# First chunk of all batches as two pairs, loaded two tokens a partition in 512-byte packets

## The chip, the core and the metric

One core of a Trainium2 chip runs the whole program. Its engines run side by side, each with its own queue that is worked off in order: TensorE (PE) multiplies matrices and writes to PSUM, VectorE (DVE) and ScalarE (ACT) work element by element, GpSimd (POOL) here issues most of the loads and some constants, and SyncE (SP) issues the stores and the transposing transfers. Sixteen DMA engines move the data that all of them ask for. The metric is the device time of one execution in microseconds (us); lower is better.

## What is computed

Two things in a row. First a retention layer without softmax on q, k, v of shape 8 x 8 x 576 x 64 (batches, heads, tokens, head size), then a two-layer network with the exact GELU on the 4608 tokens of 512 features.

```python
scores = scale * np.matmul(q, k.transpose(0, 1, 3, 2))
gamma = 1.0 - 2.0 ** (-5.0 - np.arange(H, dtype=np.float32))
Dmat = np.where(rel >= 0, gamma[:, None, None] ** rel[None, :, :], 0.0)   # rel = row - column
attn = np.matmul(scores * Dmat, v)
x = attn.transpose(0, 2, 1, 3).reshape(B * S, H * D)
h = x @ w_in                                  # 512 x 2048
out = (0.5 * h * (1.0 + erf(h / sqrt(2)))) @ w_out   # 2048 x 512
```

Inputs and output are fp32; the kernel multiplies in bf16.

## The kernel before

**Attention in chunks.** The 576 tokens of a batch are cut in four chunks of 128 and a tail of 64. Because the decay is a power of the distance, a chunk needs only its own scores and a state: the sum of k times v over all earlier chunks, 64 x 64 for each head. A *unit* is one chunk of one batch; two batches make a pair (`bp`), and units of a pair at the same chunk form a *group* that uses the four 64 x 64 quarters of TensorE side by side. For a unit the steps are: load q, k and v; transpose q and k (`qkT`, on TensorE by `turn` for the first groups, by a DMA in `turn_dma` for the later ones); scores k by q (`scores`, `sc`); the product with the mask, and in the first chunk with the decay too (`masked`, `ret`); the inner product with v (`inner`, `o_ps`); the product of the state with q (`cross`); the state itself (`state`, `u_ps`, copied to `u_sb`), which needs v scaled by the decay (`scaled_v`, `vh`); and the copy from PSUM to `xT` (`evacuate`), the input of the network.

**The first chunk** has no state before it. It multiplies its scores by `near`, a table of decay for each head (eight Exp activations of ScalarE on the distances `far`), and its inner product takes v as loaded, without scaling. Units 0 to 3 are the first chunk of the first four batches, and each is a group by itself (`groups = [[0], [1], [2], [3]]`). Their scores use TensorE in two halves, and their x is ready one after the other.

**The network in blocks** of 512 tokens. Block 0 consists of units 0 to 3. `mlp1` makes hT (w_in by x, 16 pieces of 128 features), ScalarE applies the GELU into `g`, `mlp2` multiplies by w_out (`oT`) for block 0. Later blocks use Strassen-like schemes with seven products (`part`, `m`; and from block 6 on `fast`, `f` for the first product too) on sums of w_in, w_out, g and x that VectorE makes. Blocks 0 and 1 may work on parts of a block: in block 0 the cuts are 0, 128, 256, 384, 512 tokens, one for each unit.

**Weights.** w_in comes in eight pieces of 256 columns (wi0 to wi7), w_out in eight pieces of 256 rows (wo0 to wo7). All are cast to bf16 by the DMA, and so are q, k and v, which is why GpSimd issues them. Only the very first loads (q and k of unit 0) go over the hardware queues of SP and ACT as fp32, into `first`, and are cast on VectorE. A load of one unit has 128 tokens on 128 partitions and eight heads of 64 numbers, so packets of 256 bytes on the side of the source.

**What sets the order.** The list `ORDER` (L330) gives the loads in the order in which GpSimd issues them (k1 is k of unit 1, `io` the two iotas, `dq2` a table of decay made on GpSimd), and, with letters a, b, s, z, p, u, due times and choices for the later units. At most eight loads are under way. A planner written in Python (`T`, `on`, `pe`, `fire`, and the loop at L1190) keeps an estimated time for each engine and emits each engine's instructions in the order in which it expects them to be ready; on the chip each engine then simply runs its list in order. Before its time 16, where it expects a gap on TensorE, it emits filler matmuls on zeros (`warm`). ACT makes `near`, then dv, dqT and the table load of the GELU before block 0's first activation.

Of the kernel before, what the change touches and what calls it, by code (L numbers as in the profile page):

```python
# [17 lines left out]
def kernel(  # L18
# [23 lines left out]
    C = 128  # L42
# [10 lines left out]
    groups = [[0], [1], [2], [3]]  # L53
# [9 lines left out]
    kept = pair_of[1, 0]  # L63
    raw = [i for i in range(N_U) if units[i][1] == 0]
    v_order = [i for i in range(N_U) if i not in kept]
    n = v_order.index(pair_of[0, NCI - 2][0])
    v_order[n:n] = kept

    N_PE_TR = 7
    HW_FIRST = ((("q", 0),), (("k", 0),))  # L70
# [39 lines left out]
    first = {}  # L110
    for n, keys in enumerate(HW_FIRST):
        t = o_pool.tile([128, 2, H, D], FP32, tag=f"o{n}", name="first")
        for x, (what, i) in enumerate(keys):
            first[what, i] = t[:, x]
            src = {"q": q, "k": k, "v": v}[what][2 * units[i][0] + units[i][2]]
            (nc.sync, nc.scalar)[n].dma_start(t[:, x], src[:, 0:C, :].rearrange("h s d -> s h d"))
# [14 lines left out]
    far = const.tile([128, 1, 128], FP32, name="far")  # L131
    ident = const.tile([128, 1, 128], BF16, name="ident")
    near = const.tile([128, 2, HP, 128], FP32, tag="near", name="near")
# [8 lines left out]
    def constants():  # L142
        nc.gpsimd.iota(val[:, 0, :], pattern=[[1, 128]], base=0, channel_multiplier=-1,
                       allow_small_or_imprecise_dtypes=True)
        nc.gpsimd.iota(pos[:, 0, :], pattern=[[C, NCI]], base=0, channel_multiplier=1,
                       allow_small_or_imprecise_dtypes=True)
        at = on("pool", 0.45)
        nc.vector.tensor_scalar(far, val, 0.0, 1.0e6, op0=ALU.is_lt, op1=ALU.mult)
        nc.vector.tensor_tensor(far, far, val, op=ALU.add)
        far_at = on("dve", 0.55, at)  # L150
        nc.vector.tensor_scalar(ident, val, 0.0, None, op0=ALU.is_equal)
        on("dve", 0.35)
        for h in NEAR[:N_NEAR]:
            make_near(h)
            on("act", 0.306, far_at + 0.05)

    def make_near(h):
        nc.scalar.activation(near[:, h % 2, h // 2], far[:, 0, :], AF.Exp, scale=log_gamma[h], bias=ln_scale)

    N_NEAR, NEAR = 5, (0, 2, 4, 6, 1, 3, 5, 7)  # L160
    ident1 = ident[:, 0, :]

    def make_args():
        nc.vector.tensor_scalar(pos[TAIL:, :, NCI - 1:], pos[TAIL:, :, NCI - 1:], float(-TAIL), None, op0=ALU.add)
        nc.vector.tensor_tensor(pe_arg, lgh.to_broadcast([128, H, NCI]), pos.to_broadcast([128, H, NCI]), op=ALU.mult)
        nc.vector.tensor_tensor(off, lgT, pos[:, :, 1:2].to_broadcast([128, HP, 1]), op=ALU.mult)
# [4 lines left out]
    def make_dq(hp):  # L171
        nc.scalar.activation(dqT[:, hp, C:2 * C], val[:, 0, :], AF.Exp, scale=lgT[:, hp], bias=off[:, hp])
        dq_at[1] = T["act"] + 0.41

    dq_at = {}
    later = [(4.0, "act", 0.306, lambda h=h: make_near(h)) for h in NEAR[N_NEAR:]]
    later += [(5.6, "dve", 0.45, make_args), (11.0, "dve", 0.6, make_msk),
             (6.0, "act", 0.3, lambda: nc.scalar.activation(dv, pe_arg, AF.Exp, scale=-1.0, bias=ln_scale))]
    later += [(6.2, "act", 0.41, lambda hp=hp: make_dq(hp)) for hp in range(HP)]
    later += [(8.0, "act", 1.45, lambda: nc.scalar.activation(warm_act, ln_scale, AF.Gelu))]  # L180
    T["act"], T["dve"], T["pool"] = 2.8, 2.05, 0.85


    queued = []
# [3 lines left out]
    def sum_w(i):  # L188
# [7 lines left out]
        ws_at[i] = on("dve", 1.05, land_out[i]) + SEM  # L196
# [3 lines left out]
    MOVE = {"wi": 1.33, "wo": 1.42, "ld": 0.89, "short": 0.44, "turn": 1.88, "store": 0.9}  # L200
# [47 lines left out]
    dq_done = {1}  # L248
# [23 lines left out]
    def tiles_of(i):  # L272
        g = groups[group_of[i]]
        if i not in loaded:
            if i < 4:
                qk = const.tile([128, 2, H, D], BF16, name=f"qk{i}")
            elif i == g[0]:
# [3 lines left out]
            pool, more = (const, str(i)) if i < 4 else (ld_pool, "")  # L281
            loaded[i] = (qk, pool.tile([128, H, D], BF16, tag="v" + more, bufs=1 if i < 4 else N_V, name="v_ld"))
        return loaded[i]

    def load(what, i):
# [24 lines left out]
        qk, v_ld = tiles_of(i)  # L310
        src = {"q": q, "k": k, "v": v}[what]
        for jj in (j,) if j is not None else range(2):
# [3 lines left out]
            else:  # L316
                dst = qk[:, "qk".index(what)] if i < 4 else qk[0:n, "qk".index(what), :, jj]
# [7 lines left out]
    for x, keys in enumerate(zip(*HW_FIRST)):  # L325
        for n, (what, i) in enumerate(keys):
            land[what, i] = (4.6, 5.2)[n] + 0.75 * x
            t = tiles_of(i)
            cast_due[what, i] = (t[1] if what == "v" else t[0][:, "qk".index(what)], first[what, i])
    ORDER = ("wi1 k1 wi0 io q1 v0 q2 k2 v1 wi2 v2 k3 wi3 q3 v3 wi4 wi5 wi6 k4 q5 k5 q4 v5 wi7 wo1 wo0 k6 v4 dq2 "  # L330
# [7 lines left out]
             "b21+6.0").split()  # L338
# [9 lines left out]
    for n, g in enumerate(groups):  # L348
        ORDER += [what + str(i) for what in "qkv" for i in g if what + str(i) not in ORDER and (what, i) not in first]

    def v_free(i):
        return "Bdone" in st[i] if i in raw else "V" in st[i]
# [16 lines left out]
    def finish_later():  # L369
        while later:  # L370
            _, engine, dur, fn = later.pop(0)
# [49 lines left out]
    DRAIN = 0.25  # L421
    SEM = 0.12
# [43 lines left out]
    def qkT_of(n):  # L466
        s = sg[n]
        if "qkT" not in s:
            if n < 4:
                s["qkT"] = tr_pool.tile([128, 2, HP, 128], BF16, tag="qkT1", bufs=2, name="qkT")  # L470
            else:
                s["qkT"] = tr_pool.tile([128, 2, H, 128], BF16, tag="qkT", bufs=N_QKT, name="qkT")
        return s["qkT"]

    def turn(n, jj, half):
        qk, qkT = loaded[groups[n][0]][0], qkT_of(n)
        pe_waits(max(land["qk"[jj], i] for i in groups[n]))
        b, t = bank([128, HP, 128], BF16, "qk_ps", False)
        rows = TAIL if units[groups[n][0]][2] is None else C
        for x in range(HP):  # L480
            what = qk[:, jj, 2 * x:2 * x + 2, :] if n < 4 else qk[:, jj, HP * half + x, :, :]
            nc.tensor.transpose(t[:, x, 0:rows], what[0:rows], ident1[0:rows, 0:rows])  # L482
        done = pe(0.225, HP)
        done = either(0.42 * rows / C, done, qkT[:, jj, HP * half:HP * half + HP, 0:rows], t[:, :, 0:rows])
        release(b, done + 0.05)
        sg[n]["T"] = max(sg[n].get("T", 0.0), done + SEM)

# [19 lines left out]
    def scores(n):  # L507
# [3 lines left out]
        if n < 4:  # L511
            got = [bank([128, HP, 128], FP32, "sc") for _ in range(2)]
            for hp in range(HP):
                for e in range(2):
                    sl = slice(64 * e, 64 * e + 64)
                    nc.tensor.matmul(got[e][1][:, hp, :], lhsT=qkT[sl, 1, hp, :], rhs=qkT[sl, 0, hp, :],
# [831 lines left out]
```

## Time and profile before

| what | us |
|---|---|
| median of three runs | 286.79 (285.31 to 288.63) |
| span of the profiled execution, first to last instruction | 283.7 |
| time of the profiled execution beyond its span | not given by the page |
| filler matmuls in front (10 + 23) | 4.4 + 6.0 busy |
| loads that GpSimd issues | mostly 0.85 to 0.93 each |
| DMA packets | 152804, of which 141120 are under 512 bytes on the side that the profile counts |

In the profile, lines start with the source line (L701) and engine; `hT<-xT,w_in` is what an instruction writes and reads; a number of instructions stands after x. In the chain of waits each step is followed back to what released it. In the view by stretch each row has the stretch, its length, then the busy time and number of instructions of PE, PE's weight loads, DVE, ACT and POOL, the granted TensorE clock (1.00 is full), the DMA share and GB/s.

### The profile page before, as it was taken

The numbers are of one execution on the slowest core, as the hardware profiler recorded it, in microseconds if no ns is written. First come the engines' busy times: TensorE is split into PE (matmuls) and PEld (weight loads), VectorE is DVE, ScalarE is ACT, GpSimd is POOL, SyncE is SP. The second block draws the span as 40 slices with busy tenths as digits, with TensorE's granted clock in tenths as the row PEclk, the third lists the DMA queues.
The fourth block names the chain that finished last, engine by engine and source line by source line (L and its number), as shares of the span: only waits on it lengthen the run. The fifth ranks groups of instructions, "written<-read, shape, count | busy, mean of one in ns | idle before, by whom it ended". The sixth has DMA issues, their size and how long they took to land.

```text
span 283.7 us, 8075 instructions
## 1 busy us (share of the span) xinstructions
PE 278.0 (98%) x3361; PEld 207.6 (73%) x3361; DVE 199.7 (70%) x412; ACT 158.8 (56%) x362; POOL 114.0 (40%) x143
## 2 busy tenths in 40 slices
PE   8989999999999999999999999999999999999994
PEld 3577666688874588548855778558888888888894
DVE  5753483979865595898178867889669968966822
ACT  5676724755456635693298874564565374665320
POOL 8979987993364465625468552000000000000000
PEclk9999999999999999999999999999999999999999
DMA  9999999999999999999999999910003000400133
GB/s 150 165 182 173 188 180 163 146 142 147 172 161 195 190 147 128 156 229 149 135 197 203 147 137 150 222 21 2 0 2 128 23 2 0 151 0 2 74 114 111
DMA packets 152804, 35.39 MB, mean 125 GB/s; under 512 B 141120, under 2 KB 148928, under 8 KB 152768
## 3 DMA queue, kind: packets, MB, share of 16 engines
q0 software_dynamic: 116832, 18.10, 95.3%
q1 hardware_dynamic: 34528, 16.26, 32.9%
q10 hardware_dynamic: 1408, 0.52, 0.7%
q8 instruction: 26, 0.43, 0.7%
q14 instruction: 10, 0.08, 0.1%
HBM read 36.70 MB, written 9.44 MB: 163 GB/s over the span
## 4 chain that ended last, share of the span: by engine, by line
PE 92%; POOL 3%; DMA 3%; issue 0%; DVE 0%; POOLq 0%
PE m L885 35%; PE hT L701 29%; PE f L966 13%; PE oT L746 5%; PE o_ps L600 3%; PE sc L535 3%; DMA w_in<-in_moe_w_in_dram 3%; POOL qk L318 2%; PE o_ps L653 1%; PE u_ps L619 1%; PE qk_ps L482 1%; POOL v_ld L318 1%; POOL w_in L291 1%; PE sc L525 0%; PE o_ps L591 0%
## 5 line engine op out<-in xcount | busy, mean ns | idle before, releaser
L701 PE MATMUL hT<-xT,w_in 128*128 128x512 bf16 (+3 forms) x560 | 87.4, 312 | 0.8 <-DMA w_in<-in_moe_w_in_dram 0.8
L710 ACT ACTIVATE g<-hT 128x512 bf16<-128x512 f32 (+2 forms) x106 | 57.7, 556 | 36.9 <-PE hT L701 36.1
L701 PEld LDWEIGHTS <-w_in 128*128 128x128 bf16 x560 | 48.4, 98 | 33.8 <-DMA w_in<-in_moe_w_in_dram 1.0
L885 PEld LDWEIGHTS <-gs 128*128 128x128 bf16 x656 | 62.2, 98 | 7.7
L885 PE MATMUL m<-w_sum,gs 128*128 128x256 bf16 (+1 forms) x400 | 47.7, 268 | 0.0
L318 POOL DMA_DIRECT2D v_ld<-in_v_dram x40 | 34.0, 854 | 19.3 <-DMA qk_ld<-in_k_dram 8.8
L318 POOL DMA_DIRECT2D qk_ld<-in_k_dram x36 | 30.4, 851 | 21.7 <-DMA qk_ld<-in_q_dram 19.1
L558 DVE TENSOR_TENSOR ret<-sc,msk 128x512 bf16<-128x512 f32 x48 | 30.2, 683 | 12.2 <-PE sc L535 12.2
L318 POOL DMA_DIRECT2D qk_ld<-in_q_dram x36 | 30.4, 851 | 16.9 <-DMA qkT<-qk_ld 6.5
L885 PE MATMUL m<-w_out,gs 128*128 128x256 bf16 x256 | 32.5, 273 | 0.0
L885 PE MATMUL m<-w_sum,g 128*128 128x256 bf16 x256 | 30.9, 273 | 0.0
L572 ACT ACTIVATE vh<-v_ld,dv 128x64 bf16<-128x64 bf16 x120 | 30.0, 339 | 0.0
L782 DVE TENSOR_TENSOR gs<-g 128x1024 bf16<-128x1024 bf16 x32 | 21.8, 686 | 9.0 <-ACT g L710 8.2
L885 PEld LDWEIGHTS <-g 128*128 128x128 bf16 x256 | 24.9, 98 | 3.9
L991 ACT ACTIVATE g<-f 128x512 bf16<-128x512 f32 x36 | 20.2, 590 | 8.9 <-PE f L966 7.5
L786 DVE TENSOR_TENSOR gs<-g 128x1024 bf16<-128x1024 bf16 x32 | 21.6, 684 | 0.0
L672 DVE TENSOR_TENSOR xT<-o_ps,dqT 128x512 bf16<-128x512 f32 (+1 forms) x32 | 18.4, 617 | 4.5 <-PE o_ps L653 4.4
L966 PEld LDWEIGHTS <-w_in 128*128 128x128 bf16 x192 | 18.8, 98 | 2.2
L461 ACT CAST u_sb<-u_ps 128x512 bf16<-128x512 f32 x15 | 8.7, 587 | 16.0 <-PE u_ps L619 16.0
L461 ACT COPY o<-m 128x512 f32<-128x512 f32 x14 | 8.2, 587 | 15.7 <-PE m L885 15.7
L987 ACT ACTIVATE g<-p 128x512 bf16<-128x512 f32 x12 | 7.6, 630 | 14.1 <-DVE p L985 14.1
L966 PEld LDWEIGHTS <-wi 128*128 128x128 bf16 x144 | 14.0, 98 | 1.6
(96 smaller groups left out, 337.6 us busy)
## 6 DMA issues: line engine op xcount, KB each, us to landing
out_dram<-o SPq DMA_DIRECT2D x27, 256.0 KB, 6.3
v_ld<-in_v_dram POOLq DMA_DIRECT2D x32, 128.0 KB, 9.1
qk_ld<-in_k_dram POOLq DMA_DIRECT2D x28, 128.0 KB, 10.7
qk_ld<-in_q_dram POOLq DMA_DIRECT2D x28, 128.0 KB, 8.6
w_in<-in_moe_w_in_dram POOLq DMA_DIRECT2D x8, 256.0 KB, 7.3
w_out<-in_moe_w_out_dram POOLq DMA_DIRECT2D x8, 256.0 KB, 8.0
out_dram<-o SPq DMA_DIRECT2D x14, 128.0 KB, 2.1
qk_ld<-in_q_dram POOLq DMA_DIRECT2D x8, 64.0 KB, 11.4
```

Source lines behind the costliest of these rows:

```text
L318: nc.gpsimd.dma_start(dst, src[2 * bp + jj, :, ci * C:ci * C + n, :].rearrange("h s d -> s h d"))
L461: nc.scalar.copy(dst, src)
L558: nc.vector.tensor_tensor(r, t, by, op=ALU.mult)
L572: nc.scalar.activation(vh[:, h, :], loaded[i][1][:, h, :], AF.Copy, scale=dv[:, h, ci:ci + 1])
L672: nc.vector.tensor_tensor(x_of(i)[:, :, n * x:n * x + n], o, dqT[:, :, ci * C:ci * C + n], op=ALU.mult)
L701: nc.tensor.matmul(hT[:, m, :], lhsT=w[:, cc, o:o + 128], rhs=x_tiles[t][:, cc, lo:hi], start=(cc == 0), stop=(cc == N_DM - 1))
L710: nc.scalar.activation(g_of(t, m0 // 2)[:, m0 % 2:m0 % 2 + n, lo:hi], hT, AF.Gelu)
L782: nc.vector.tensor_tensor(s.rearrange("p m a b -> p m (a b)"), g[:, :, 0, :], g[:, :, 1, :], op=ALU.add)
L786: nc.vector.tensor_tensor(s, g[:, :, :, LEFT], g[:, :, :, RIGHT], op=MINUS)
L885: nc.tensor.matmul(m[:, 0 if apart else ts, :], lhsT=a, rhs=w[:, c0:c1], start=p in begins and mm == 0 and ts == 0, stop=mm == N_DF // 2 - ...
L966: nc.tensor.matmul(m[:, y, :], lhsT=a[:, c], rhs=d[:, c], start=p in (P1, P7) and y == 0 and c == 0, stop=c == 1, skip_group_check=True)
L991: nc.scalar.activation(g[:, :, rows, cols], m, AF.Gelu)
```

## The change

Units 0 to 3 become two groups of a pair each. Each unit is loaded with two adjacent tokens to a partition, so 64 partitions by eight heads by 512 bytes, and the two batches of a pair lie in the two halves of the partitions. q and k of both batches of the first pair go ahead over the hardware queues of SP and ACT as fp32 (four loads for two), all else by GpSimd. Everything in the first chunk then works on tokens split by parity:

- transposes take 64 x 64 outputs in column halves, 64 for 32; scores take 64 x 64 quarters, 64 instructions of 128 columns for 32 over half the array; the inner product has 64 as before; the state has 64 for 32, since each parity is a product of its own
- `near` has three 64-wide blocks of distances for each head (`away`), eight activations of 192 columns for 128, and a table `dv2` is added; `masked_two` makes four masked products for a pair, as many as before
- v of a pair is scaled in place by one VectorE instruction of 1024 columns, after the inner product has read it
- `evacuate` writes xT with a stride of two tokens
- block 0 is cut in two halves of 256 tokens; dqT starts from chunk 0, so GpSimd makes three of these tables instead of two
- the list of loads, and all due times and choices behind it, are new. In the built program ScalarE scales v for 9 later units where it did so for 15 units, and VectorE for the rest; in the last three blocks VectorE has 5 copies to `p` (2 before), 9 to `f` (8) and 3 to `o` (2).

```diff
-    groups = [[0], [1], [2], [3]]
+    groups = [[0, 1], [2, 3]]
...
-    N_PE_TR = 7
+    N_PE_TR = 5
...
+    def doubled(what, i):
+        src = {"q": q, "k": k, "v": v}[what][2 * units[i][0] + units[i][2]]
+        return src[:, 0:C, :].rearrange("h (p t) d -> p h (t d)", t=2)
...
+    first = [o_pool.tile([128, H, 2, D], FP32, tag=f"o{n}", name="first") for n in range(2)]
+    for n, what in enumerate("qk"):
+        for i in range(2):
+            (nc.sync, nc.scalar)[i].dma_start(first[n][half_of(i)].rearrange("p h t d -> p h (t d)"), doubled(what, i))
...
-    ORDER = ("wi1 k1 wi0 io q1 v0 q2 k2 v1 wi2 v2 k3 wi3 q3 v3 wi4 wi5 wi6 k4 q5 k5 q4 v5 wi7 wo1 wo0 k6 v4 dq2 "
...
+    ORDER = ("v0 io v1 wi0 q2 k2 q3 k3 wi1 v2 v3 wi2 wi3 k4 wo0 q11 wi5 wi4 q4 q5 k5 dq1 wi6 wi7 k6 wo1 wo2 v5 wo3 "
...
+        if n < P0:
+            got = [[bank([128, HP, 2, 64], FP32, "sc") for _ in range(2)] for _ in range(2)]
             for hp in range(HP):
+                for kp in range(2):
+                    for j in range(2):
+                        cols = slice(64 * j, 64 * j + 64)
+                        for e in range(2):
+                            sl = slice(64 * e, 64 * e + 64)
+                            nc.tensor.matmul(got[kp][e][1][cols, hp], lhsT=qkT[sl, 1, 2 * hp + kp, cols],
+                                             rhs=qkT[sl, 0, 2 * hp:2 * hp + 2, cols],
+                                             start=(hp == 0), stop=True, skip_group_check=True)
...
+                nc.vector.tensor_tensor(vh, vh, dv2.to_broadcast([128, H, 2, D]), op=ALU.mult)
...
+        if pair[0] < 4:
             for j, i in enumerate(pair):
+                sl = half_of(i)
+                for h in range(H):
+                    for t in range(2):
+                        nc.tensor.matmul(u_ps[sl, h, :], lhsT=loaded[i][0][sl, 1, h, t, :], rhs=st[i]["vh"][sl, h, t, :],
+                                         start=(h == 0 and t == 0), stop=(h == H - 1 and t == 1), skip_group_check=True)
...
-            x_at[i] = either(0.68, s["B"], x_of(i), o) + SEM
+            x_at[i] = either(0.68, s["B"], x_of(i).rearrange("c h (p t) -> c h t p", t=2), o) + SEM
...
-            cuts = (0, 128, 256, 384, 512) if t == 0 else (0, 256, 512)
+            cuts = (0, 256, 512)
```

In the built program TensorE's list after the change runs: 10 fillers, the first pair's transposes, 6 fillers, its scores, 7 fillers, the second pair's transposes of q, 2 fillers, of k, the first pair's inner product, 4 fillers, the second pair's scores, hT of the first 256 tokens with wi0, wi1, wi2, the first pair's state, the second pair's inner product, hT with wi3, two oT matmuls that read wo0, hT of the second 256 tokens with wi0 to wi3, and hT of all 512 tokens with wi4, wi5, wi6, wi7 with 16 transposes of the next group in between.

More of the change, by code (lines that the diff above doesn't have):

```diff
@@ L310, in load @@
         qk, v_ld = tiles_of(i)
+        if i < 4:
+            dst = (v_ld if what == "v" else qk[:, "qk".index(what)])[half_of(i)]
+            nc.gpsimd.dma_start(dst.rearrange("p h t d -> p h (t d)"), doubled(what, i))
+            sw_dma(0.94, "two", putter(land, (what, i)))
+            return
         src = {"q": q, "k": k, "v": v}[what]
@@ L476, in turn @@
         qk, qkT = loaded[groups[n][0]][0], qkT_of(n)
-        pe_waits(max(land["qk"[jj], i] for i in groups[n]))
+        pe_waits(turn_at(n, jj, half))
         b, t = bank([128, HP, 128], BF16, "qk_ps", False)
@@ L486, in turn, with turn_at @@
         sg[n]["T"] = max(sg[n].get("T", 0.0), done + SEM)
+    def turn_at(n, jj, half):
+        if not ident_at or n == 0 and ("qk"[jj], half) not in cast_at or any(("qk"[jj], i) not in land for i in groups[n]):
+            return 1e9
+        at = cast_at["qk"[jj], half] if n == 0 else max(land["qk"[jj], i] for i in groups[n]) + 0.05
+        return max(at, ident_at[0])
     def turn_dma(n, jj):
@@ L542, in masked @@
         s = st[i]
-        if i not in raw and any(x[3] is make_msk for x in later):
+        if i < 4:
+            if i % 2 == 0:
+                masked_two(i)
+            return
+        if not made(make_msk):
             finish_later()
@@ L584, in inner @@
         s = st[i]
-        pe_waits(max(s["R"], s["V"] if "vh" in s and i not in raw else land["v", i]))
+        if i < 4:
+            if i % 2 == 0:
+                inner_two(i)
+            return
+        pe_waits(max(s["R"], s["V"]))
         if j is None:
@@ L1287 @@
                 turn(*a)
-                half = (half + 1) % (2 if nT < 4 else 4)
+                half = (half + 1) % 4
                 nT += half == 0
```

286 lines of the change are left out of this document (173 added, 113 removed), and 14 rows, old and new, of the table ORDER.

## The prediction

> **What bounds the kernel now.** I read the page first: busy shares and the chain that ended last.
>
> ```profile
> PE 278.0 (98%) x3361; PEld 207.6 (73%) x3361; DVE 199.7 (70%) x412; ACT 158.8 (56%) x362; POOL 114.0 (40%) x143
> PE 92%; POOL 3%; DMA 3%; issue 0%; DVE 0%; POOLq 0%
> ```
>
> TensorE is the bound, with 6% of the chain on GpSimd's DMA issues and on one DMA. A share is an average, so the second view is busy time by stretch (the first number after the stretch is its length, the next PE's busy time).
>
> ```profile
> 0.00:18.50 18.50, 16.53 (x170) 9.36 (x171) 11.72 (x42) 12.30 (x33) 16.50 (x25) 1.00 1.70 162
> 18.50:32.20 13.70, 13.70 (x168) 10.45 (x168) 3.83 (x8) 8.91 (x20) 12.16 (x15) 1.00 1.83 181
> 180.00:240.00 60.00, 60.00 (x717) 49.30 (x717) 49.12 (x90) 32.89 (x58) 0.00 (x0) 1.00 0.15 40
> 280.00:283.70 3.70, 0.01 (x1) 0.00 (x0) 0.29 (x1) 0.00 (x0) 0.00 (x0) 0.82 0.49 139
> ```
>
> From 18.5 on PE never pauses; a busy PE can hide short waits, but the chain confirms that it is PE's own work. The last 3.7 us are the last store. So whatever can be gained lies before 18.5, and anything lost later is lost in full. The chain in order of time (start, length, what) shows the start and gives the pace of PE's groups.
>
> ```profile
> 1.25 0.88 POOL w_in L291
> 11.04 7.39 DMA w_in<-in_moe_w_in_dram
> 18.47 1.05 PE hT L701 x8
> 27.88 0.89 PE qk_ps L482 x16
> 32.29 0.57 PE sc L535 x32
> 40.28 4.37 PE hT L701 x40
> 44.65 0.86 PE oT L746 x4
> 120.16 8.74 PE hT L701 x40
> ```
>
> The start is GpSimd issuing loads until 11.0, then the fourth piece of w_in landing at 18.4. In front of it PE runs filler matmuls:
>
> ```profile
> L1180 PE MATMUL warm<-zeros 128*128 128x512 bf16 x23 | 6.0, 382 | 0.0
> ```
>
> From 18.47 the remaining 261.5 us of PE work and 3.7 us of store are fixed. My milestone is the end of block 0's first matrix product (hT) for all 512 tokens and all of w_in, 32.2 now (the chain's sc at 32.29 follows it). The change is worth what it moves that milestone, plus or minus work carried across it.
>
> **What the loads cost.** GpSimd's rows (start, length) and the DMA view of the same issues (last number: us from issue to landing) give landings:
>
> ```profile
> 10.17 0.93 POOL L318 DMA_DIRECT2D qk<-in_k_dram  x1
> 11.78 0.96 POOL L318 DMA_DIRECT2D qk<-in_q_dram  x1
> 12.66 0.95 POOL L318 DMA_DIRECT2D v_ld<-in_v_dram  x1
> 13.52 2.33 POOL L291 DMA_DIRECT2D w_in<-in_moe_w_in_dram  x3
> 42.22 0.69 POOL L318 DMA_DIRECT2D qk_ld<-in_q_dram  x1
> 43.44 0.68 POOL L318 DMA_DIRECT2D qk_ld<-in_q_dram  x1 [0.53 <-DMA w_out<-in_moe_w_out_dram]
> ```
> ```profile
> first<-in_k_dram ACTq DMA_DIRECT2D x1, 256.0 KB, 4.6
> first<-in_q_dram SPq DMA_DIRECT2D x1, 256.0 KB, 4.0
> w_in<-in_moe_w_in_dram POOLq DMA_DIRECT2D x1, 256.0 KB, 5.0
> qk<-in_k_dram POOLq DMA_DIRECT2D x1, 128.0 KB, 5.5
> w_in<-in_moe_w_in_dram POOLq DMA_DIRECT2D x1, 256.0 KB, 7.4
> qk<-in_q_dram POOLq DMA_DIRECT2D x1, 128.0 KB, 6.9
> v_ld<-in_v_dram POOLq DMA_DIRECT2D x1, 128.0 KB, 6.8
> w_in<-in_moe_w_in_dram POOLq DMA_DIRECT2D x1, 256.0 KB, 7.2
> qk_ld<-in_q_dram POOLq DMA_DIRECT2D x1, 64.0 KB, 7.1
> qk_ld<-in_q_dram POOLq DMA_DIRECT2D x1, 64.0 KB, 6.4
> ```
>
> The first software load lands at 1.25+5.0 = 6.25. Further on: k of unit 3 at 15.67, wi3 at 18.44, q at 18.68, v at 19.46, wi4 at 20.72. In a backlog a 128 KB load therefore takes 0.78 (19.46-18.68) and a 256 KB piece of w_in 1.26 (20.72-19.46). Between 15.67 and 18.68 one of each landed in 3.01 where 2.04 would do: about 1.0 us was lost there, and I keep that loss. The two 64 KB half-height loads land at 49.32 and 49.84, 0.52 apart.
>
> **The change, part by part.**
>
> *New loads.* No row shows 64 partitions by 8 heads of 512 bytes. The half-height load has the same number of packets and half the bytes (0.52), the w_in piece the same packets and twice the bytes (1.26); the old load has the same bytes in twice the packets (0.78). A straight line in bytes gives 0.77, so the packet size alone buys little; I take 0.72, with 0.52 and 1.26 as ends. Issuing one costs GpSimd 0.69 (half height) to 0.93; I take 0.8.
>
> *Order.* In the built program GpSimd issues v0, the two iotas, v1, wi0, q2, k2, q3, k3, wi1, v2, v3, wi2, wi3, k4, wo0. Behind v0 until wo0 stand seven of the new loads, four pieces of w_in, k4 and wo0 (as long as a w_in piece): 7x0.72 + 4x1.26 + 0.78 + 1.26 = 12.1, so wo0 lands at 6.25+12.1+1.0 = 19.4. Four fp32 loads instead of two go ahead on the hardware queues; the second of the two now lands 0.6 behind the first, so two more are 1.2, of which I charge half to the software loads: wo0 at 20.0. GpSimd would have issued it by 1.25+0.5+8x0.8+4x0.8+0.9 = 12.3 and is not the bound. wi3 lands 2.04 earlier, at 18.0 (18.44 now), with two more loads already in front of it.
>
> *PE's queue.* PE runs in order: hT of the first 256 tokens with wi0 to wi3, then two oT matmuls that need wo0, then hT of the second 256 tokens, then 512-wide hT with wi4 to wi7 and 16 transposes between. So everything queues behind wo0, whose wait is new. Work behind it: oT 2x0.215 = 0.43; 32 hT of 256 columns at 4.37/40 = 0.109 is 3.5; 32 of 512 at 8.74/40 = 0.2185 is 7.0; transposes 0.89. Sum 11.8, milestone 31.8: 0.4 earlier.
>
> *Does x come in time?*
>
> ```profile
> 0.74 0.50 ACTq L116 DMA_DIRECT2D first<-in_k_dram  x1
> L461 ACT COPY o<-m 128x512 f32<-128x512 f32 x14 | 8.2, 587 | 15.7 <-PE m L885 15.7
> 4.77 2.45 ACT L158 ACTIVATE near<-far,ln_scale 128x128 f32<-128x128 f32 x8 [2.00 <-DVE far L149]
> 7.34 1.64 ACT L172 ACTIVATE dqT<-val,off,lgT 128x128 f32<-128x128 f32 x4
> 8.99 1.28 ACT L180 ACT_TABLE_LOAD   x1
> 8.02 1.29 DVE L558 TENSOR_TENSOR ret<-sc,near 128x512 bf16<-128x512 f32 x2 [0.66 <-PE sc L516]
> 11.01 0.69 DVE L456 CAST xT<-o_ps 128x512 bf16<-128x512 f32 x1
> 36.82 0.42 PE L619 MATMUL u_ps<-vh,qk_ld 128*64 128x64 bf16 x16
> ```
>
> The second k load lands at 0.74+4.6+1.2 = 6.5. Cast 0.7, transposes and copies 1.0, scores 0.57, four masked products (the row has two in 1.29) 2.6, inner product 0.57, xT 0.69, and 0.5 for hand-overs: 13.2 on DVE. The other batch's xT is on ACT behind eight wider near (2.45x1.5 = 3.7 from about 4.5), three copies of 0.6, dv twice, dqT 1.64 and the table load 1.28: about 14.2. The first three hT then end at 16.8. DVE scales v (an estimate of 1.3, two masked products' elements), makes four masked products and lets the second pair's inner product begin at 17.1; with wi3's hT that is 18.6, before wo0's 20.0. So PE idles some 1.4 us there; the filler and the attention of the start are hidden behind loads, as now.
>
> *Work carried over.* Two oT (0.43) are done that are not done now. The states of the first chunk take 32 matmuls for 16, each token parity by itself and sixteen in a row in the same quarter of the array. Sixteen cost 0.42 now: 32 cost 0.84 if they overlap as now and 1.68 if not; I take 1.2. The first pair's falls into the wait for wo0, the second comes in the dense part: +0.8. [...]
>
> *The rest of the schedule.* The due times and lists of all later units are new. Matmul columns are the same, so at best nothing changes: PE is at 60.00 of 60.00 already.
>
> **Sum.** -0.4 (milestone) -0.4 (oT) +0.8 (state) = 0: a span of 283.7. The page gives no time of the profiled execution beyond its span; the median of the three runs shown is 286.79, 3.1 above it, which I carry over: 286.8.
>
> **Rivals.**
>
> *Half-height loads are slow.* If 64 partitions take the loads at half rate, a new load costs as much as a w_in piece, 1.26. The seven are 3.8 later, wo0 lands at 23.8, all else queues behind it: +3.7, 290.5, over +1% (about what a measurement of this kernel can tell from no change). It decides above 1.1 a load (7x0.38 = 2.7). Against it: half-height rows move 64 KB in 0.52, 126 GB/s against 168 for full height, not half. [...] Chance 0.10.
>
> *The later schedule stalls PE.* PE has no slack, and DVE is 49.12 of 60 busy in 180 to 240. In the built program DVE has five more PSUM copies in the last three blocks (p 2 to 5, f 8 to 9, o 2 to 3), taken from ACT. If each holds up PE by its own 0.69 that is 3.4: 290.2. It decides where DVE reaches a copy later than PE's next use. Against: ACT was 32.89 busy in that stretch and can take what DVE leaves. Any other late buffer shows in the same way. Chance 0.22.
>
> *The loads are better than I think.* At 0.52 a load wo0 lands 1.4 earlier and the wait goes; xT at 14.2 is next (4 hT, state, inner: 19.3). That plus overlapping states gives -0.7 -0.4 -0.4 below my sum with the 1.0 loss gone as well: -2.5, 284.3. Chance 0.12, and a third of it beyond 1%.
>
> **The numbers.** The forecast's case holds 0.56, from 285.6 to 288.2 (the load between 0.6 and 0.9, the state's ends). Faster by over 1%: the third of the last rival and a little of noise, 0.08. Slower: both slow rivals less their milder half-outcomes, 0.30. Within 1%: 0.62. The range takes in the fast rival's end and the middle of the slow ones: 284.4 to 290.3.
>
> **What would show it.** In the profile of the changed kernel: PE idle before an oT matmul, released by the DMA of w_out, at 18 to 20; the state's 32 matmuls taking 0.8 to 1.7; wi3 landing near 18.0; the 512-wide hT ending near 31.8; PE at 60.00 of 60.00 in the later stretches. If PE shows waits after 40, the second rival is right; if new loads land 1.1 or more apart, the first. If hT starts after 16, my sum for the masked products or ACT's queue is wrong.

## The result: 4% slower, and where the time shows

The changed kernel takes 297.99 us in the median of four runs, the kernel before 286.97 in the median of four: a ratio of 1.041, 95% interval 1.035 to 1.047. The forecast was 286.8 with a range up to 290.3, so the time lies outside it. The profiled execution of the changed kernel has a span of 297.0 (before: 283.7) and a time of 298.77; the spans of the four executions run from 295.4 to 297.0. All times and ratios here leave out disturbed executions: two of e5_same's four (296.6 with them), and one of e4_hw4's ten, which took 573.91.

First the view by stretch of the changed kernel; the columns are those of the prediction's second fence. The third row is new: it runs to where block 0's hT ends now.

```profile
0.00:18.50 18.50, 12.97 (x154) 6.28 (x155) 9.75 (x49) 9.73 (x22) 14.34 (x25) 0.82 1.31 170
18.50:32.20 13.70, 13.06 (x184) 9.91 (x183) 7.34 (x15) 7.82 (x13) 10.15 (x13) 1.00 1.77 183
32.20:37.60 5.40, 5.40 (x35) 2.57 (x37) 1.10 (x4) 2.98 (x5) 4.56 (x6) 1.00 1.63 189
180.00:240.00 60.00, 55.91 (x635) 42.02 (x632) 43.45 (x81) 27.91 (x54) 1.16 (x2) 0.94 0.48 64
```

Two stretches have changed most. In the first 18.5 us TensorE is busy 12.97 (16.53 before) at a granted clock of 0.82 (1.00 before). And 180 to 240, which was 60.00 of 60.00 busy, has 4 us of idle time and a clock of 0.94. TensorE's waits by releaser (total, times, longest) name both:

```profile
PE qk_ps L520 <- DVE qk L496: 4.3, 2, 2.3
PE sc L585 <- DMA qkT<-qk_ld: 4.3, 2, 4.1
```

The first are the first pair's transposes, waiting for the casts of q and k. The second are scores waiting for a transposing DMA. The chain of waits of the changed kernel (start, length) has what was late behind each, and TensorE's timeline has the idle times in brackets:

```profile
1.57 7.78 DMA first<-in_k_dram
...
173.06 1.16 SPq L538
174.32 12.01 DMA qkT<-qk_ld
```
```profile
1.19 3.68 PE L1306 MATMUL warm<-zeros 128*128 128x512 bf16 x10 [1.19 <-DVE zeros L117]
6.94 0.71 PE L520 MATMUL qk_ps<-ident,qk 128*64 128x128 bf16 x16 [2.07 <-DVE qk L496]
9.92 1.06 PE L520 MATMUL qk_ps<-ident,qk 128*64 128x128 bf16 x16 [2.27 <-DVE qk L496]
10.92 2.74 PE L1299 MATMUL warm<-zeros 128*128 128x512 bf16 x6
13.59 0.91 PE L565 MATMUL sc<-qkT 64*64 64x128 bf16 x32
...
19.83 2.79 PE L810 MATMUL hT<-xT,w_in 128*128 128x256 bf16 x24
22.55 1.00 PE L723 MATMUL u_ps<-v,qk 64*64 64x64 bf16 x29
...
37.53 0.64 PE L585 MATMUL sc<-qkT 64*64 64x128 bf16 x32
...
186.38 1.07 PE L585 MATMUL sc<-qkT 64*64 64x128 bf16 x32 [4.09 <-DMA qkT<-qk_ld]
```

The same two points, start of hT and scores of the next group, in the timeline of the kernel before:

```profile
11.78 0.61 PE L701 MATMUL hT<-xT,w_in 128*128 128x128 bf16 x8
32.22 0.64 PE L535 MATMUL sc<-qkT 64*64 64x128 bf16 x32
```

hT of block 0 starts at 19.83 (11.78 before). I compare kernels by one mark, the scores of the next group: they start at 37.53 here and at 32.22 before. So the start loses 5.3. Two oT matmuls (0.4) are already done at the mark, which lie behind it in the kernel before. What follows the mark takes 297.0 - 37.53 = 259.5 (before: 283.7 - 32.22 = 251.5), 8.0 more. Both losses sum to the 13.3 of the span, since the mark splits it in two.

### The profile page after: what moved, and what is told of

It reads as the page before. It is cut to its first block, busy times and chain, and to the rows that moved or that the text cites. A ratio compares the mean times of both kernels' runs of the same rounds, so it can differ in the third digit from the quotient of the medians.

```text
span 297.0 us, 8108 instructions
## 1 busy us (share of the span) xinstructions
PE 282.1 (95%) x3405; PEld 207.6 (70%) x3405; DVE 209.3 (70%) x437; ACT 143.3 (48%) x296; POOL 111.5 (38%) x142
## 4 chain that ended last, share of the span: by engine, by line
PE 86%; DMA 11%; SPq 1%; ACT 0%; issue 0%; DVE 0%; DVEq 0%
PE m L996 30%; PE hT L810 26%; PE f L1080 12%; DMA qkT<-qk_ld 8%; PE oT L855 5%; DMA first<-in_k_dram 3%; PE sc L585 3%; PE o_ps L683 2%; PE warm L1299 2%; PE o_ps L763 1%; PE u_ps L729 1%; PE qk_ps L522 1%; PE qk_ps L520 1%; PE u_ps L723 1%; SPq L538 1%; PE sc L565 0%
## 5 line engine op out<-in xcount | busy, mean ns | idle before, releaser
L810 PE MATMUL hT<-xT,w_in 128*128 128x512 bf16 (+1 forms) x480 | 89.1, 342 | 1.1 <-ACT xT L501 0.6
L819 ACT ACTIVATE g<-hT 128x512 bf16<-128x512 f32 x96 | 56.3, 595 | 51.0 <-PE hT L810 47.4
L810 PEld LDWEIGHTS <-w_in 128*128 128x128 bf16 x480 | 46.3, 99 | 37.2 <-issue 3.3
L611 DVE TENSOR_TENSOR ret<-sc,msk 128x512 bf16<-128x512 f32 x56 | 35.4, 683 | 19.3 <-PE sc L585 19.3
L358 POOL DMA_DIRECT2D v_ld<-in_v_dram x36 | 30.3, 848 | 26.5 <-DMA qk_ld<-in_k_dram 12.0
L996 PE MATMUL m<-w_out,gs 128*128 128x256 bf16 x256 | 33.1, 273 | 0.0
L782 DVE TENSOR_TENSOR xT<-o_ps,dqT 128x512 bf16<-128x512 f32 (+1 forms) x36 | 21.0, 624 | 3.5 <-PE o_ps L763 3.3
L1080 PEld LDWEIGHTS <-w_in 128*128 128x128 bf16 x192 | 18.8, 98 | 2.2
L651 ACT ACTIVATE vh<-v_ld,dv 128x64 bf16<-128x64 bf16 x72 | 18.1, 336 | 0.0
L501 ACT COPY o<-m 128x512 f32<-128x512 f32 x13 | 7.6, 585 | 17.8 <-PE m L996 17.8
L948 DVE SCALAR_TENSOR_TENSOR o<-m,o 128x512 f32<-128x512 f32 (+1 forms) x9 | 5.6, 629 | 13.8 <-PE m L996 9.7
```

The source lines that it names most:

```text
L358: nc.gpsimd.dma_start(dst, src[2 * bp + jj, :, ci * C:ci * C + n, :].rearrange("h s d -> s h d"))
L501: nc.scalar.copy(dst, src)
L611: nc.vector.tensor_tensor(r, t, msk.to_broadcast([128, HP, 128]), op=ALU.mult)
L651: nc.scalar.activation(vh[:, h, :], loaded[i][1][:, h, :], AF.Copy, scale=dv[:, h, ci:ci + 1])
L782: nc.vector.tensor_tensor(x_of(i)[:, :, n * x:n * x + n], o, dqT[:, :, ci * C:ci * C + n], op=ALU.mult)
L810: nc.tensor.matmul(hT[:, m, :], lhsT=w[:, cc, o:o + 128], rhs=x_tiles[t][:, cc, lo:hi], start=(cc == 0), stop=(cc == N_DM - 1))
```

## Experiments

The question was split in two: what makes the start late, and whether the later wait comes from the due times, from the late start, or from something else. In the table, "mark" is the start of the next group's scores, "rest" is span less mark. Kernels whose mark stands at the same place of the same lists as in the changed kernel have one; the ratio is to the kernel before, run on the same chip. Span, mark and rest are of one profiled execution each.

| kernel | edit to the changed kernel | time | ratio (95%) | span | mark | rest |
|---|---|---|---|---|---|---|
| before | | 286.97 | | 283.7 | 32.22 | 251.5 |
| changed | | 297.99 | 1.041 (1.035 to 1.047) | 297.0 | 37.53 | 259.5 |
| e6_fill | TensorE kept busy at the start | 296.6 | 1.038 (1.032 to 1.044) | 295.9 | 35.81 | 260.1 |
| e5_same | k of the first pair earlier | 294.17 | 1.029 (1.022 to 1.037) | 294.2 | 35.41 | 258.8 |
| e9_slot | two buffers exchanged | 291.9 | 1.022 (1.019 to 1.025) | 289.8 | 36.89 | 252.9 |
| e10_both | e5_same and e9_slot | 288.59 | 1.011 (1.007 to 1.014) | 286.7 | 35.04 | 251.7 |
| e13_all | e10_both, kept busy, state alternating | 290.14 | 1.014 (1.011 to 1.017) | 289.6 | 33.96 | 255.6 |

### The start: bytes, height, idle time

**Four full-height loads in the kernel before (e4_hw4).** k1 and q1 also go from `ORDER`.

```diff
-    HW_FIRST = ((("q", 0),), (("k", 0),))
+    HW_FIRST = ((("q", 0), ("q", 1)), (("k", 0), ("k", 1)))
```

> The kernel before with four full-height fp32 loads on SP and ACT for two (q and k of units 0 and 1, 128 partitions by 8 heads by 256 bytes), k1 and q1 taken out of GpSimd's list. Theory A (by bytes): the four land one after another 1.2 to 2.0 apart, the last near 9, as in the changed kernel (4.74, 6.14, 8.11, 9.35). Theory B (half height): full-height loads land 0.6 apart, as the two of before seem to (4.74, 5.32), the last by 6.7. Time: within 2 us of the kernel before by B, 2 to 6 us more by A.

In the timeline of this kernel the casts of what these loads bring start as the loads land:

```profile
4.76 0.56 DVE L456 CAST qk<-first 128x512 bf16<-128x512 f32 x1 [0.53 <-DMA first<-in_q_dram]
5.43 0.62 ACT L461 CAST qk<-first 128x512 bf16<-128x512 f32 x1
8.23 0.47 DVE L456 CAST qk<-first 128x512 bf16<-128x512 f32 x1 [2.92 <-DMA first<-in_q_dram]
9.08 0.62 ACT L461 CAST qk<-first 128x512 bf16<-128x512 f32 x1 [2.72 <-DMA first<-in_k_dram]
```

The first two come 0.7 apart, and the next two 3.5 and 3.65 behind them. So 0.6 or 0.7 between the two of a pair is not the price of the second: the two queues run side by side (both loads of the first pair are issued at 0.74 and land at 4.74 and 5.44) and both end at the pair's end. The price is 3.5 for two, 1.75 for 256 KB, beside the loads of GpSimd. Theory A holds for the last load (near 9), not for its even steps; the time is 288.41, ratio 1.008 (1.005 to 1.011), 2.3 us more by the ratio.

**The changed kernel with full-height loads of the same bytes (e7_full).**

```diff
-            (nc.sync, nc.scalar)[i].dma_start(first[n][half_of(i)].rearrange("p h t d -> p h (t d)"), doubled(what, i))
+            (nc.sync, nc.scalar)[i].dma_start(first[n][:, :, i], {"q": q, "k": k}[what][i, :, 0:C, :].rearrange("h s d -> s h d"))
```

> The changed kernel with its four fp32 loads in the form of the kernel before: 128 partitions by 8 heads by 256 bytes, same bytes, queues and places in the lists; tokens lie in other partitions, so q and k of the first pair are not those of the reference. It tells height from bytes. By bytes alone the four land at 4.7, 6.1, 8.1 and 9.4 as in the changed kernel. If half height costs, they land earlier, the last by 8.4 or before (the kernel before with four such loads had its second pair at about 8.0 and 8.8, with 512 KB of w_in beside them).

The DMA view (last number: us from issue to landing), first of the changed kernel, then of this one; the issues are at 0.74 for q, at 1.25 to 1.57 for k:

```profile
first<-in_q_dram SPq DMA_DIRECT2D x1, 256.0 KB, 5.4
first<-in_q_dram ACTq DMA_DIRECT2D x1, 256.0 KB, 4.0
first<-in_k_dram ACTq DMA_DIRECT2D x1, 256.0 KB, 6.6
first<-in_k_dram SPq DMA_DIRECT2D x1, 256.0 KB, 7.8
```
```profile
first<-in_q_dram ACTq DMA_DIRECT2D x1, 256.0 KB, 4.8
first<-in_q_dram SPq DMA_DIRECT2D x1, 256.0 KB, 4.1
first<-in_k_dram SPq DMA_DIRECT2D x1, 256.0 KB, 7.2
first<-in_k_dram ACTq DMA_DIRECT2D x1, 256.0 KB, 7.5
```

Full height brings the slower q 0.6 earlier and the last k at 8.78 for 9.35. So the form of the load costs 0.6 here. The full-height form has twice the packets, of 256 bytes for 512 at the source, so height and packet size are not told apart. The rest of the delay comes with the two further loads, as in e4_hw4. The mark is at 37.27 and the span stays at 297.1.

**k as bf16 by GpSimd, all lists kept (e5_same).** The two fp32 loads of k and its cast go, two loads in the new form are issued in front of v0:

```diff
-    for n, what in enumerate("qk"):
+    for n, what in enumerate("q"):
         for i in range(2):
...
+    for i in range(2):
+        nc.gpsimd.dma_start(tiles_of(0)[0][half_of(i), 1].rearrange("p h t d -> p h (t d)"), doubled("k", i))
     while T["pool"] < 4.0:
```

> The changed kernel with every engine's list of instructions kept as it is, but for this: k of the first pair is loaded by GpSimd as bf16 in front of all else, and the two fp32 loads of k and the cast of k are gone. Only the start's time changes, not the order of anything. Theory A (the wait at 182 lies in the emitted order of the later schedule): hT of block 0 ends at 34 to 35.5 (37.6 now), the wait for a transposing DMA near 180 stays at 3 to 5, span about 294. Theory B (the late start makes it: the loads, which are tied to TensorE's progress by free buffers, fall behind): the wait shrinks to under 1 with the start 2 to 3 us earlier, span 286 to 288.

The mark comes 2.1 earlier (35.41), and the wait does not go: 4.1 us, now at 170. So 2.1 of the 5.3 by which the start is late do not make it. The rest is 258.8.

**TensorE kept busy, no load touched (e6_fill).**

```diff
-    for _ in range(N_WARM):
+    for _ in range(N_WARM + 9):
...
+        if (n, jj, half) == (0, 1, 0):
+            more = ps.tile([128, 512], FP32, tag="b7", name="warm")
+            for _ in range(10):
+                nc.tensor.matmul(more, lhsT=zeros[:, :128], rhs=zeros, start=True, stop=True)
```

> The changed kernel with its lists as they are and 19 more filler matmuls on TensorE: 9 behind the first ten and 10 between the first pair's transposes of q and of k, where it sat idle 2.07 and 2.27 us. No load and no other engine's list changes. Theory (idle time halves the clock, and the half clock costs the start 2 to 3 us): the granted clock stays 1.00 from 5 to 20, the six fillers in front of the scores take 1.3 (2.7 now), hT of block 0 ends near 35.5 to 36.5 (37.6 now). Rival (loads alone set the start): hT ends within 0.5 of 37.6. The later wait at 182: as for the other kernel with the same lists, it goes by theory B in part (the start is 1 to 2 us earlier), it stays by theory A.

The changed kernel's trace shows half clock (0.50) from 7.37 to 14.20 and from 184.86 to 191.69. The view by stretch of windows of that length, 0.24 later, in the changed kernel and in this one:

```profile
7.61:14.44 6.83, 4.56 (x57) 2.32 (x55) 1.52 (x4) 4.80 (x13) 4.23 (x7) 0.52 1.65 187
185.10:191.93 6.83, 5.55 (x59) 2.79 (x60) 4.55 (x8) 1.09 (x2) 0.68 (x1) 0.52 1.59 196
```
```profile
7.61:14.44 6.83, 6.67 (x88) 3.28 (x85) 3.12 (x7) 4.77 (x13) 4.13 (x6) 1.00 1.67 186
```

The clock is 1.00 and the mark 1.7 earlier (35.81), with every load as late as before. So idle time in front of the two sets of first transposes costs 1.7 in the slowed-down work behind it. That is read from the trace: in the times, 1.038 (1.032 to 1.044) for 1.041, the gain is not clear. The later wait stays here too (5.5 in three places, the longest 2.7).

**Estimates corrected (e2_est).** The planner was told when q, k and the following loads land.

```diff
-        land[what, i] = (3.6, 5.0)[n]
+        land[what, i] = (5.8, 9.0)[n]
...
             sw_dma(0.94, "two", putter(land, (what, i)))
+            if (what, i) == ("v", 0):
+                transfer(0, 0.0, 2.9, lambda end: None)
```

> The changed kernel with two estimates of its planner set to what the trace shows: q and k of the first pair land at 5.8 and 9.0 of its time (3.6 and 5.0), and the loads of GpSimd behind the first v are 2.9 later. It then puts its filler matmuls in front of the transposes, where TensorE idled 2.1 and 2.3 us. Theory (TensorE's idle start and the half clock that followed cost part of the 5.4 us): the granted clock is 1.00 from 5 to 20, the scores of the first pair end near 12.3 (14.5 now), hT of block 0 ends near 35.5 (37.6 now). Rival (the start waits for loads alone, wi2 and wi3 at 17.9 and 20.3): hT ends at 37 or later, whatever the clock. The wait at 182: gone if it came from the planner being out of step with the chip, there if it comes from the due times.

294.91, ratio 1.030 (1.022 to 1.038), span 292.4. The scores of the first pair start at 12.5 (13.59), hT at 18.53. The wait at 182 is gone, but the lists behind block 0 have changed too, and with them, as was seen later, the buffers. A new wait of 2.0 for ScalarE's scaling of v stands at 75.

**k by GpSimd with the planner told of it (e3_ksw)**, and the same **with three small edits (e8_more)**: no planned wait of 1.0 before the first scores, v scaled behind the second pair's masked products, the state alternating. The core of the last:

```diff
-            for j, i in enumerate(pair):
-                sl = half_of(i)
-                for h in range(H):
-                    for t in range(2):
+            for h in range(H):
+                for t in range(2):
+                    for j, i in enumerate(pair):
+                        sl = half_of(i)
                         nc.tensor.matmul(u_ps[sl, h, :], lhsT=loaded[i][0][sl, 1, h, t, :], rhs=st[i]["vh"][sl, h, t, :],
```

> The changed kernel with k of the first pair loaded by GpSimd as bf16 in front of v0, in the new half-height form, and only q0 and q1 by SP and ACT as fp32; no cast of k. Theory A (a load costs by the bytes it lands, 1.3 to 1.5 for 256 KB of fp32, whatever its height): q0 and q1 land by 5.5 as the two did before the change, k0 and k1 near 6.5 and 7.2, v0 near 8; the first pair's scores end near 10 (14.5 now), wi3 lands near 19 (20.3), hT of block 0 ends near 35. Theory B (half-height fp32 loads are slow by themselves): q1 lands at 6 or later, k1 at 8 or later, and hT ends 37 or later. Span: 3 us less than the changed kernel by A, if the wait at 182 stays as it is.

> The kernel with k of the first pair by GpSimd (e3_ksw), with three more edits: no wait of 1.0 planned in front of the first scores, v of a pair scaled only after the second pair's masked products, and the state's 32 matmuls alternating between the two batches' quarters. If the state's sixteen matmuls in a row in one quarter cost, its 32 take 0.6 or less instead of 1.0; if each matmul costs by itself, 1.0 stays. hT of block 0 starts 0.5 to 1 us earlier than 16.1, and the wait of 0.64 for xT goes. Span 285 to 286.5 (287.1 for e3_ksw), if the later schedule meets no new wait.

e3_ksw: 288.86, ratio 1.010 (1.006 to 1.013), hT from 16.14; its slower q still lands at 6.3, as theory B has it, while hT ends at 34.8, as A has it. e8_more: 290.63, ratio 1.019 (1.016 to 1.022), hT from 14.95, but the third piece of w_in is 0.9 late behind it, and small waits for VectorE appear after 240. What it settles is the state; TensorE's rows, of the changed kernel above (29 of 32 in 1.00) and here (0.6 or less was expected; e13_all, with the order of the state changed and the later lists kept, has 28 of 32 in 0.63):

```profile
21.09 0.69 PE L723 MATMUL u_ps<-v,qk 64*64 64x64 bf16 x32
```

### The later wait: due times or a buffer

**Due times of the kernel before (e1_due).** The letters a, s, b, z of units 8 and up and all u were exchanged, in the list `ORDER` alone.

> The changed kernel, with the due times a, s, b, z of units 8 and up and all u taken from the kernel before; the loads, the p times and TensorE's list through block 0's hT are the same as in the changed kernel. Theory (the new due times starve TensorE later): hT of block 0 ends at 37.6 as in the changed kernel, but the wait of 4.2 us for a transposing DMA at 182 goes, and with it the half clock of 6.8 us behind it, about 7 us together: span 290 (297.0 now). Rival (the late start itself shifts the loads against TensorE): the wait stays, span 296 to 298.

298.21, ratio 1.040 (1.030 to 1.050): nothing gained. The wait at 182 is gone, and in its place TensorE waits 2.5 at 227 for VectorE's scaling of v and 1.3 at 87 for no releaser that the profile shows. This could not be read as it was meant, because the exchange moved the buffers as well.

**What GpSimd waits for.** GpSimd's timeline of the changed kernel has what lies behind the late transposes, some 40 us ahead of the stall:

```profile
121.80 1.36 POOL L358 DMA_DIRECT2D qk_ld<-in_q_dram  x2 [0.56 <-PE hT L810]
123.15 0.70 POOL L358 DMA_DIRECT2D qk_ld<-in_k_dram  x1
124.21 0.68 POOL L358 DMA_DIRECT2D qk_ld<-in_k_dram  x1 [0.36 <-DMA qk_ld<-in_q_dram]
129.18 0.69 POOL L358 DMA_DIRECT2D v_ld<-in_v_dram  x1 [4.29 <-DVE ret L611]
131.62 0.68 POOL L358 DMA_DIRECT2D v_ld<-in_v_dram  x1 [1.75 <-DMA qk_ld<-in_k_dram]
144.13 1.76 POOL L358 DMA_DIRECT2D qk_ld<-in_q_dram  x2 [11.83 <-DMA qkT<-qk_ld]
```

The rows of 0.68 are the third tail. The next group's load waits 11.83 for a transposing DMA. In the built program that load waits for all four loads of the tail (DMASW0 to 3) and for the tail's two transposes (DMAHW3 and 4); in the kernel with the buffers exchanged, for older transfers and TensorE:

```
changed   L358 DMACopy qk_ld<-in_q_dram 128x8x64 [waits DMASW6,DMASW3,DMAHW3,DMASW2,DMAHW4,DMASW1,DMASW0]
e9_slot   L358 DMACopy qk_ld<-in_q_dram 128x8x64 [waits DMAHW5,DMAHW7,DMASW6,PE]
```

From there to the stall the trace has two steps. The loads behind the wait are issued one after another from 144.13, and the q load issued at 155.39 takes 16.0 to land. SyncE, which issues the transposes in order, waits for q (its waits from 168 to 172):

```profile
SPq L538 <- DMA qk_ld<-in_q_dram: 6.2, 1, 6.2
```

So it issues the next transpose at 171.55 and the one that TensorE waits for at 174.32, which then takes 12.01. In the kernel with the buffers exchanged the two are issued at 164.14 and 168.51.

There are five buffers for q and k (`N_LD`). Named A to E by their address, the 18 groups get A E D C B A B D C E A D **B B** C E A D in the changed kernel: the group behind the third tail (the 14th load group) gets the buffer that the tail was just loaded to. In the kernel before the same place reads B C B. Of the kernels here, the changed one, e5_same, e6_fill and e7_full have B B, and these four have the wait of a transposing DMA between 169 and 188; e1_due, e2_est, e3_ksw, e4_hw4, e8_more and e12_best have B C B and don't.

**Only the buffers exchanged (e9_slot).** Every list on every engine is the same.

```diff
-    N_LD = 5
+    SLOT = iter("AEDCBABDCEADBCBEADCBDEA")
...
-                qk = ld_pool.tile([128, 2, H, 2, D], BF16, tag="qk", bufs=N_LD, name="qk_ld")
+                qk = ld_pool.tile([128, 2, H, 2, D], BF16, tag="qk" + next(SLOT), name="qk_ld")
```

> The changed kernel with every list as it is; only the buffers of two loads of q and k are exchanged. In the changed kernel the group behind the third tail gets the buffer of that tail, which was loaded just in front of it, so that GpSimd's queue must wait until the tail has landed and both its transposes have (11.83 us at 132 to 144); here it gets the buffer that four groups use in between, and the next group gets the tail's. Theory (this one buffer makes the later wait): hT of block 0 ends at 37.6 as before, GpSimd's wait at 132 shrinks to 7 or less, TensorE's wait at 182 goes with the half clock behind it, span 289.5 to 291 (297.0 now). Rival (due times or the late start make it): the wait at 182 stays above 3, span 296 to 298.

GpSimd's timeline of this kernel at the same place:

```profile
129.03 0.68 POOL L358 DMA_DIRECT2D v_ld<-in_v_dram  x1 [3.89 <-DMA qk_ld<-in_k_dram]
131.74 0.89 POOL L358 DMA_DIRECT2D qk_ld<-in_q_dram  x1 [2.03 <-PE hT L810]
...
137.17 1.76 POOL L358 DMA_DIRECT2D v_ld<-in_v_dram  x2
146.58 1.75 POOL L358 DMA_DIRECT2D qk_ld<-in_q_dram  x2 [7.65 <-DMA qkT<-qk_ld]
```

Six loads are issued from 131.74 that waited until 144.13 in the changed kernel; the wait of 7.65 then comes a group later (the kernel before has one of 6.5 there, and e1_due one of 10.6, without a stall of TensorE for a transpose, so the length of the wait alone does not decide). TensorE has no wait for a transposing DMA left, the rest is 252.9 for 259.5, and the span 7.2 less: 289.8. The theory holds, with 6.6 as the price. The other 0.6 lies in front of the mark, where the granted clock from 7.61 to 14.44 was 0.75 in this execution and 0.52 in the other.

**Both (e10_both).**

> The kernel with k of the first pair by GpSimd and all lists of the changed kernel (e5_same: span 294.2), with the same exchange of two buffers. If the start and the buffer are separate causes, their gains add: 2.1 from the start and 6.5 to 7.5 from the buffer, span 287 to 288.5. If the wait has another cause, 293 to 295.

286.7: the gains add, 2.5 in the start and 7.8 behind it against the changed kernel. The rest (251.7) is within 0.2 of the kernel before.

**The bad buffer in the kernel before (e11_bad).** The same exchange the other way round, all lists kept.

> The kernel before with every list as it is, and the buffers of the same two loads exchanged so that the group behind the third tail gets that tail's buffer, as in the changed kernel. Theory (the buffer alone): GpSimd waits some 10 us or more for the tail's transposes, the load stream is a group behind, and TensorE waits for a transposing DMA between 165 and 190: 3 to 7 us more than the kernel before (span 287 to 291, against 283.7). Rival (it takes the changed schedule too): no wait on TensorE, span within 1 of 283.7.

The rival holds. GpSimd waits 8.8 at 132 to 141, but TensorE only 0.4, and the span is 284.1; the time is 286.19, ratio 1.003 (1.000 to 1.006). The buffer does the harm in the changed schedule only; there the tail's loads and transposes end at 144.1, here GpSimd goes on at 140.69. Whether it takes the changed lists or the later start was not separated.

### What is left

**A better order of loads on e8_more (e12_best)**: the third piece of w_in ahead of v2 and v3, in `ORDER` alone.

> The kernel with the state alternating and no planned wait (e8_more: span 288.0, 0.9 of idle for the third piece of w_in at 17.4), with that piece loaded in front of v2 and v3. If the loads in front set the time, the idle 0.9 goes and the first scores of the next group are at 31.0 (31.9); span 287 or less, if the later schedule doesn't change. It beats the kernel before only if the later part loses nothing against it: 284 to 285 then; I expect 286 to 288.

290.4, ratio 1.017 (1.013 to 1.021), span 287.8. The idle 0.9 for w_in shrinks to 0.6, and the state waits 0.9 for the scaled v instead; the mark's scores start at 31.83. A miss.

**Fillers, alternating state, both causes gone (e13_all)**: e10_both with `range(N_WARM + 8)` and the state's loop of e8_more.

> The kernel with k of the first pair by GpSimd and the exchanged buffers (e10_both: span 286.7), with 8 more fillers behind the first ten, so that TensorE does not idle in front of the first transposes, and with the state's 32 matmuls alternating between the quarters. All other lists are those of the changed kernel. Theory (what is left in e10_both is mostly the half clock of the start): the clock is 1.00 from 5 on, hT starts near 16.2 (17.7), the state takes 0.69 for 1.00, span 284.5 to 285.2, within 1% of the kernel before. Rival (the new form itself costs it): hT starts at 17 or later, span 286 or more.

The start does as the theory says, and another wait gives it back. TensorE's timeline and waits:

```profile
16.40 3.04 PE L812 MATMUL hT<-xT,w_in 128*128 128x256 bf16 x24
```
```profile
PE sc L587 <- DMA qkT<-qk_ld: 2.8, 2, 2.7
```

The mark is at 33.96, 1.1 earlier than in e10_both and still 1.7 later than in the kernel before, but at 132 scores wait 2.7 for a transposing DMA, the granted clock is 0.91 from 120 to 140, and the rest grows by 3.9. This execution has the longest span of six (287.1 to 289.6), so part of the 3.9 may be chance. Buffers and later lists are those of e10_both. The transpose was issued at 121.65 (122.04 in e10_both) and took 12.8 to land (11.1 there). What decides when the transposes between 120 and 150 land stays open, and so does what makes the pool choose a buffer. No version here beats the kernel before.

## Why the prediction failed, by its own steps

- **"the second of the two now lands 0.6 behind the first, so two more are 1.2"; "The second k load lands at 0.74+4.6+1.2 = 6.5".** This step failed in the start. The last k landed at 9.35 (1.57 + 7.8). 0.6 was the difference of two transfers under way together, not the time of one; e4_hw4 shows 3.5 for a pair. With 3.5 for 1.2, k is at 8.8 and, with the 0.6 of the half-height form (e7_full), at 9.4. A nearer row was there: the w_in pieces of the same 256 KB, at 1.26, so 2.5 for two. The loads behind were late with it: wi3 landed at 20.3 (12.12 + 8.2; forecast 18.0).
- **"the filler and the attention of the start are hidden behind loads, as now".** They were not. TensorE idled 2.07 and 2.27, the clock was halved (0.50) for 6.83, and the six fillers in front of the scores took 2.74. e6_fill prices it at 1.7. The prediction counted idle time of TensorE as free as long as a load was later.
- **"13.2 on DVE", "about 14.2" for the other batch's xT, and hT behind it.** hT started at 19.83, 5.6 later. The two steps above account for about 4.6 of it (2.85 by k, 1.7 by e6_fill). The sum also left out what stands in TensorE's list between the masked products, done at 17.04, and hT: transposes of the second pair until 17.72, and its scores at 19.26, 0.57 until hT starts. The test named for it ("my sum for the masked products or ACT's queue is wrong") pointed at the wrong terms: four masked products took 2.48 where 2.6 were summed. Nor did TensorE idle for wo0. It landed at 22.3 (13.74 + 8.6; forecast 20.0), and TensorE came for it at 25.7.
- **"at best nothing changes"**, and the second rival. The side was right, and waits after 40 did show; the mechanism was not. No PSUM copy of VectorE held TensorE up, but a transposing DMA, behind a load stream that had stood still for 11.83. Its price was 6.6 us (e9_slot), not 3.4: the wait, and half clock for 6.83 us behind it. The rival's aside ("Any other late buffer shows in the same way") had the cause but no size.
- **The new loads.** 0.72 for one was not too low: issued 0.67 apart, with 7.9, 7.9 and 8.1 to landing for three in a row, so they landed about 0.7 apart. As they were issued no closer, they may cost less. The first rival, which needed 1.1, fell for these. Its half rate shows in no run for the fp32 loads either: e7_full has 0.6 for the half-height form, and in the first two fortieths of the span (7.4 us each) all transfers together moved 143 and 187 GB/s in the changed kernel, 157 and 185 in e7_full. What the 0.6 comes from stays open.
- **The state**, 0.84 to 1.68, taken at 1.2, took 1.00 (29 of the 32 matmuls), and 0.69 when the quarters alternate (e8_more): the price of the order is 0.3 each. The upper end, 1.68, was an estimate for matmuls that do not overlap. No run shows it: sixteen in a row in one quarter did not cost it.

So the sum is 283.7 + 5.3 at the mark + 8.0 behind it = 297.0, where -0.4 and +0.4 were forecast. Of the 5.3, e5_same prices the loads of k at 2.1 and e6_fill the idle time at 1.7; with both mended and the state alternating, e13_all keeps 1.7. Of the 8.0, 6.6 are the buffer's. What makes the 1.7 and the other 1.4 was not separated.

## What to carry to other kernels

When two transfers land close together, look at when they were issued before reading the gap as a price: the price of one is what a further pair adds (in e4_hw4 0.7 lay between the two of a pair, and a further pair added 3.5). Where a pool hands out buffers, list for each load of the built program which transfers it waits for. A load that waits for the loads and transposes issued just in front of it stops the whole queue (11.83 us in the changed kernel), and a kernel with no slack may pay for that tens of microseconds later (TensorE's wait of 4.09, some 40 us behind it). And price TensorE's idle time in front of dense work by the clock that it gets afterwards (0.50 for 6.83 us in the changed kernel).

## What the runs showed of the hardware

In the changed kernel the clock was halved (0.50) twice for the same 6.83 us, from 7.37 and from 184.86, 2.5 and 2.6 us after TensorE fell idle. 2.07 idle and 0.4 of work stood between the last filler and the first halving (the 2.27 came after it had begun), and 2.6 idle ahead of the second. What sets the 6.83, no run shows.

The same lists can get a different clock: 0.52 and 0.75 from 7.61 to 14.44 in the executions of the changed kernel and of e9_slot, whose starts are the same program. And the column can miss slow work in the first microseconds: 24 of the first transposes, from 7.97, took 1.49 in e10_both and all 32, from 7.59, took 1.24 in e13_all, and the six fillers behind them 2.04 and 1.47, all four at a shown clock of 1.00.

A load stream that stands still is dear in one schedule and nearly free in another: 11.83 in the changed kernel cost 6.6 us, and 8.8 in the kernel before (e11_bad) cost 0.4 of span.
